# Moving weight and first input loads to time 0, and placing the first one-hot rows with VectorE, in a routed attention followed by a SiLU layer

## The chip, the cores and the metric

The kernel runs on one core of a Trainium2 chip. The metric is the device time in microseconds; the median of three runs of the kernel before is 393.85 us (393.36 to 396.67). The engines named below are TensorE (PE in the profile, with its weight loads as PEld), VectorE (DVE), ScalarE (ACT), GpSimd (POOL) and SyncE (SP, which issues DMAs). GpSimd issues DMAs as well. The profiled run, from which all views are taken, has a span of 390.8 us.

## The reference

Four batches with eight heads each, 768 positions, head dimension 64. Each head has 16 centroids; a query may look only at keys of its own cluster. The result goes, with all heads of a position side by side, through a layer with a SiLU between two matrices.

```python
q, k, v = [4, 8, 768, 64]; centroids = [8, 16, 64]; w_in = [512, 2048]; w_out = [2048, 512]   # float32

c_n = centroids / (norm(centroids) + 1e-6)          # q and k are normalized too: no effect on the argmax
q_assign = argmax(einsum('bhsd,hcd->bhsc', q_n, c_n))
k_assign = argmax(einsum('bhsd,hcd->bhsc', k_n, c_n))
mask = q_assign[:, :, :, None] == k_assign[:, :, None, :]
scores = where(mask, q @ k.T / 8, -1e9)
attn = softmax(scores)
x = (attn @ v).transpose(0, 2, 1, 3).reshape(3072, 512)
h = x @ w_in
out = (h * sigmoid(h)) @ w_out
```

## The kernel before

The kernel works on 16 pairs of heads (`p`), each with three blocks of 256 queries. Of every pair, q and k (`t` = 0 and 1) are loaded, split into two f16 halves (`hl`: the rounded value and the rest), and transposed into `abt`, whose first 64 partitions then hold the rounded values. Pairs 0 to 3 are transposed by TensorE (`turn_pe`), the later ones by a transposing DMA (`turn_dma`). The mask isn't applied to the scores. Instead, the one-hot row of each position's cluster, times 2048, is put under its 64 values, on partitions 64 to 79 of `abt`; a score matmul over 80 partitions then adds 2048 x 2048 where query and key have the same cluster, and the exponential brings the others to zero.

```python
def load(p, t):
    nat = mp.tile([128, 2, NJ * D], f32, name=f"nat{t}", bufs=3)
    nc.sync.dma_start(nat, (q, k)[t][...])

def load_v(p):
    natv = mp.tile([128, 2, NJ * D], f32, name="natv", bufs=2)
    nc.sync.dma_start(natv, v[...])

def cast_v(p):                 # f32 to f16 beside a block of ones, which gives the row sums
    for h in range(2):
        nc.gpsimd.tensor_copy(vts[p % NV][:, :, h, 0:D], natvs[p][:, h]...)

def split(p, t, part, eng=nc.vector): ...       # two VectorE operations of 128x768

def logits(pl):                # q and k against the centroids; wh and wl: two halves of the weights
    for lo, hi in ((0, 512), (512, 768)):
        psL = ps.tile([128, 512], f32, name="psL", tag="moe", bufs=3)
        for n, (w, h) in enumerate(((wh, 0), (wh, 1), (wl, 0), (wl, 1))):
            for a, p in enumerate(pl):
                for t in range(2):
                    g = 64 * a + 32 * t         # 32 rows: 16 of head 0, 16 of head 1
                    nc.tensor.matmul(psL[g : g + 32, 0 : hi - lo], w[:, p % HB, h], ab[:, h, lo:hi], ...)

def route_a(pl):   nc.vector.transpose(lt[0:n, ...], psL...)                  # blocks of 32x32
def route_b(pl):   nc.vector.tensor_reduce(out=mx[0:n], in_=lt, axis=AX.X, op=ALU.max)
def route_c(pl):   nc.vector.tensor_tensor(out=oht..., in0=lt, in1=mx..., op=ALU.is_ge)
def route_d(pl):
    nc.vector.transpose(ohu[0:n], oht)
    nc.vector.tensor_scalar(out=oh[0:n], in0=ohu[0:n], scalar1=OHV, scalar2=None, op0=ALU.mult)
def route_e(pl):               # one DMA for each head and each of q and k
    nc.sync.dma_start(ab[D : D + HC, h, :], oh[g : g + HC, :])
```

After the routing, `qk` makes scores (`st`) and exponentials (`P`), and `pv` multiplies them with v and copies the result to `osb`. The row sums go by DMA to 32 partitions (`z_out`), are inverted by VectorE (`z_recip`), go to DRAM and come back broadcast (`z_bcast`); all three DMAs are issued by GpSimd. `z_mul` makes the input `xt` of the layer, whose units are `unit_a` and `unit_b`. The main loop runs over slots: in each, a third of a unit's scores, the values of the scores of three slots before, what `at(slot, ...)` has put there, and layer units.

```python
def z_out(n):   nc.gpsimd.dma_start(zt, osbs[n][D : D + 1]...)
def z_recip(n):
    nc.vector.reciprocal(rz, zts.pop(n))
    nc.gpsimd.dma_start(rzd..., rz)
def z_bcast(n): nc.gpsimd.dma_start(rzb..., rzs.pop(n).to_broadcast([64, 2 * UQ]))
...
# the start
craw = load_centroids()
for p in range(2):
    for t in range(2):
        load(p, t)
make_identity(nc, ident)
for vt in vts:                                  # six
    nc.gpsimd.memset(vt[:, :, :, D:128], 1.0)
load_v(0)
centroid_norm(craw)
for t in range(2):
    split(0, t, 0, VE); split(0, t, 1)
... # turn_pe of pair 0
for t in range(2):
    split(1, t, 0)
centroid_rest(craw)
logits([0])
for t in range(2):
    load(2, t)
load_v(1)
split(1, 0, 1)
route_a([0]); route_b([0]); route_c([0]); route_d([0]); route_e([0])
cast_v(0)
split(1, 1, 1)
... # turn_pe of pair 1
# the weights: eight DMAs for w_in and eight for w_out, one every second slot; they cast f32 to f16
for n in range(2):
    for r in range(NR):
        wld.append(lambda r=r, o=o: nc.gpsimd.dma_start(win_s[:, r, o], win_v[:, r, o]))
for g in range(NFB // 2):
    wld.append(lambda g=g: nc.gpsimd.dma_start(wout_s[:, 2 * g : 2 * g + 2], wout_v[:, 2 * g : 2 * g + 2]))
...
at(0, lambda: cast_v(1))
at(0, lambda: (load(3, 0), load(3, 1), load_v(2)))
at(3, lambda: load_v(3))
for n, fn in enumerate(wld):
    at(1 + 2 * n, fn)
```

Of the kernel before, what the change touches and what calls it, by code (L numbers as in the profile page):

```python
# [9 lines left out]
f32 = mybir.dt.float32  # L10
f16 = mybir.dt.float16
AF = mybir.ActivationFunctionType
ALU = mybir.AluOpType
AX = mybir.AxisListType
# [3 lines left out]
def kernel(  # L18
# [10 lines left out]
    nc = tc.nc  # L29
    B, H, S, D = q.shape  # L30
    HC = centroids.shape[1]
    DM = moe_w_in.shape[0]
    DF = moe_w_in.shape[1]
    NT = B * S
    NJ = S // 128
    NFB = DF // 128
# [23 lines left out]

    wh = const.tile([128, HB, 2, 32], f16, name="wh")
    wl = const.tile([128, HB, 2, 32], f16, name="wl")
    NV = 6
    vts = [const.tile([128, NJ, 2, 128], f16, name=f"vt{n}") for n in range(NV)]

# [8 lines left out]
    def load(p, t):  # L74
        b, r = divmod(p, HB)
        nat = mp.tile([128, 2, NJ * D], f32, name=f"nat{t}", bufs=3)
        nc.sync.dma_start(nat, (q, k)[t][b, 2 * r : 2 * r + 2].rearrange("h (p j) d -> p h (j d)", j=NJ))
        nats[p, t] = nat

    def load_v(p):  # L80
        b, r = divmod(p, HB)
        natv = mp.tile([128, 2, NJ * D], f32, name="natv", bufs=2)
        nc.sync.dma_start(natv, v[b, 2 * r : 2 * r + 2].rearrange("h (p j) d -> p h (j d)", j=NJ))
        natvs[p] = natv

    def cast_v(p):
        for h in range(2):
            nc.gpsimd.tensor_copy(vts[p % NV][:, :, h, 0:D], natvs[p][:, h].rearrange("p (j d) -> p j d", d=D))

    def split(p, t, part, eng=nc.vector):  # L90
        nat = nats[p, t].rearrange("p h (j d) -> p (h j) d", d=D)
        if part == 0:
            hl = hls[p, t] = mp.tile([128, 2 * NJ, 2, D], f16, name="hl", bufs=3)
            eng.tensor_scalar(out=hl[:, :, 0, :], in0=nat, scalar1=128.0, scalar2=None, op0=ALU.mult)
        else:
            hl = hls[p, t]
            nc.vector.scalar_tensor_tensor(  # L97
                out=hl[:, :, 1, :], in0=nat, scalar=128.0, in1=hl[:, :, 0, :], op0=ALU.mult, op1=ALU.subtract
            )
# [21 lines left out]
    def logits(pl):  # L121
        tl = []
# [5 lines that stand above are left out]
                        g = 64 * a + 32 * t  # L128
                        ab = abts[p][:, t].rearrange("p (h j) c -> p h (j c)", h=2)
                        nc.tensor.matmul(  # L130
                            psL[g : g + 32, 0 : hi - lo], w[:, p % HB, h], ab[:, h, lo:hi], start=(n == 0), stop=(n == 3)
                        )
            tl.append(psL)
        psls[pl[0]] = tl

    def route_a(pl):
        n = 64 * len(pl)
        lt = mp.tile([128, S], f32, name="lt", bufs=1)
        tl = psls.pop(pl[0])
        nc.vector.transpose(lt[0:n, 0:512], tl[0][0:n])  # L140
        nc.vector.transpose(lt[0:n, 512:768], tl[1][0:n, 0:256])
        lts[pl[0]] = lt

    def route_b(pl):
        n = 64 * len(pl)
        lt = lts[pl[0]][0:n].rearrange("p (a c) -> p a c", c=HC)
        mx = mp.tile([128, S // HC], f32, name="mx", bufs=2)
        nc.vector.tensor_reduce(out=mx[0:n], in_=lt, axis=AX.X, op=ALU.max)  # L148
        mxs[pl[0]] = mx

    def route_c(pl):
        n = 64 * len(pl)
        lt = lts.pop(pl[0])[0:n].rearrange("p (a c) -> p a c", c=HC)
        oht = mp.tile([128, S], f16, name="oht", bufs=1)
        nc.vector.tensor_tensor(  # L155
            out=oht[0:n].rearrange("p (a c) -> p a c", c=HC), in0=lt,
            in1=mxs.pop(pl[0])[0:n].unsqueeze(2).to_broadcast([n, S // HC, HC]), op=ALU.is_ge,
        )
        ohts[pl[0]] = oht

    def route_d(pl):
        n = 64 * len(pl)
        ohu = mp.tile([128, S], f16, name="ohu", bufs=1)
        nc.vector.transpose(ohu[0:n], ohts.pop(pl[0])[0:n])  # L164
        oh = mp.tile([128, S], f16, name="oh", bufs=2)
        nc.vector.tensor_scalar(out=oh[0:n], in0=ohu[0:n], scalar1=OHV, scalar2=None, op0=ALU.mult)
        ohs[pl[0]] = oh

    def route_e(pl):
        oh = ohs.pop(pl[0])  # L170
# [3 lines that stand above are left out]
                    g = 64 * a + 32 * t + HC * h  # L174
                    ab = abts[p][:, t].rearrange("p (h j) c -> p h (j c)", h=2)
                    nc.sync.dma_start(ab[D : D + HC, h, :], oh[g : g + HC, :])  # L176


    K = D + HC
# [103 lines left out]
    def centroid_norm(craw):  # L283
        csq = mp.tile([128, D], f32, name="csq")
        nc.vector.tensor_tensor(out=csq, in0=craw, in1=craw, op=ALU.mult)
        nc.vector.tensor_reduce(out=cs, in_=csq, axis=AX.X, op=ALU.add)
        nc.scalar.activation(out=cy, in_=cs, func=AF.Sqrt, bias=zbias, scale=1.0)
        nc.scalar.preload_act_table(AF.Exp)
        newton()

    def centroid_rest(craw):
        newton()
        nc.vector.tensor_scalar(out=cy, in0=cy, scalar1=1e-6, scalar2=None, op0=ALU.add)
        cw = mp.tile([128, 1], f32, name="cw")
        nc.vector.reciprocal(cw, cy)
        cn = mp.tile([128, D], f32, name="cn")
        nc.vector.tensor_scalar(out=cn, in0=craw, scalar1=cw, scalar2=None, op0=ALU.mult)

        chh = mp.tile([128, D], f16, name="chh")
        nc.vector.tensor_copy(chh, cn)  # L300
        ch2 = mp.tile([128, 2, D], f16, name="ch2")
        cl2 = mp.tile([128, 2, D], f16, name="cl2")
        for n in range(2):
            nc.vector.tensor_scalar(out=ch2[:, n, :], in0=chh, scalar1=OHV, scalar2=None, op0=ALU.mult)
        for n in range(2):
            nc.vector.scalar_tensor_tensor(out=cl2[:, n, :], in0=cn, scalar=OHV, in1=ch2[:, n, :], op0=ALU.mult, op1=ALU.subtract)
        for src, dst in ((ch2, wh), (cl2, wl)):
            pt = ps.tile([128, 128], f16, name="pt", tag="moe", bufs=3)
            nc.tensor.transpose(pt, src.rearrange("p n d -> p (n d)"), ident)
            pt4 = pt.rearrange("p (r h c) -> p r h c", h=2, c=HC)  # L310
            for h in range(2):
                nc.vector.tensor_copy(dst[:, :, h, HC * h : HC * h + HC], pt4[:, :, h])


    units = []
# [10 lines left out]
    def at(slot, fn):  # L326
        events.setdefault(slot, []).append(fn)


    nc.vector.memset(zbias, 0.0)  # L330
    nc.vector.memset(bias32, -32.0)
    craw = load_centroids()
    for p in range(2):
        for t in range(2):
            load(p, t)
    make_identity(nc, ident)
    nc.vector.memset(wh, 0.0)
    nc.vector.memset(wl, 0.0)
    for vt in vts:
        nc.gpsimd.memset(vt[:, :, :, D:128], 1.0)  # L340
    load_v(0)
    AC, VE = nc.scalar, nc.vector
    centroid_norm(craw)
    for t in range(2):
        split(0, t, 0, VE)
        split(0, t, 1)
    for t in range(2):
        for h in range(2):
            turn_pe(0, t, h, AC)
    for t in range(2):  # L350
        split(1, t, 0)
    centroid_rest(craw)
    logits([0])
    for t in range(2):
        load(2, t)
    load_v(1)
    split(1, 0, 1)
    route_a([0])
    route_b([0])
    route_c([0])  # L360
    route_d([0])
    route_e([0])
    cast_v(0)
    split(1, 1, 1)
    for t in range(2):
        for h in range(2):
            turn_pe(1, t, h, AC)

    wld = []
    for n in range(2):  # L370
        for r in range(NR):
            o = slice(n * DF // 2, (n + 1) * DF // 2)
            wld.append(lambda r=r, o=o: nc.gpsimd.dma_start(win_s[:, r, o], win_v[:, r, o]))
    for g in range(NFB // 2):
        wld.append(lambda g=g: nc.gpsimd.dma_start(wout_s[:, 2 * g : 2 * g + 2], wout_v[:, 2 * g : 2 * g + 2]))


    def route(pl, x):
# [25 lines left out]
    route([1], 1)  # L404
    front_pe(2, 2)
    front_pe(3, 9)
    at(0, lambda: cast_v(1))
    at(0, lambda: (load(3, 0), load(3, 1), load_v(2)))
    at(3, lambda: load_v(3))
    at(6, lambda: cast_v(2))  # L410
    at(8, lambda: cast_v(3))
    for n, fn in enumerate(wld):
        at(1 + 2 * n, fn)
    for b in range(1, B):
        front([b * HB, b * HB + 1], 36 * b - (3 if b == 1 else 8))
        front([b * HB + 2, b * HB + 3], 36 * b + (4 if b == 1 else 2))
# [88 lines left out]
```

The softmax here doesn't subtract the row's maximum and nothing guards it: scores larger than these inputs give would overflow.

## Time and profile before

| | |
|---|---|
| median of three runs | 393.85 us |
| span of the profiled run | 390.8 us |
| PE busy | 336.5 us (86%) |
| PEld busy | 245.4 us (63%) |
| DVE busy | 248.0 us (63%) |
| ACT busy | 226.0 us (58%) |
| POOL busy | 106.0 us (27%) |
| DMA, issued by SP (q1) | 36.22 MB, 36.7% of 16 engines |
| DMA, issued by GpSimd (q0) | 10.69 MB, 13.5% of 16 engines |

Busy time is the sum of an engine's instructions. A share over the whole span says little here, as the kernel has different stages: a start with loads and routing, a stage with attention alone, and, from about 116 us on, attention and layer units together. The page shows this in forty slices of 9.77 us; each digit is a share of the slice in tenths, PEclk is TensorE's granted clock in tenths of full speed:

```profile
PE   2476965183849999999999999999999999999995
DVE  6827577465554796796755786785845364555661
PEclk9668798588887999999999999999999999999999
DMA  7663589999716179654034598645120111111111
```

TensorE is nearly always busy from the thirteenth slice on. In the seventh to the tenth slice the DMA engines are at 90% or more. The median times from issue to landing differ: 5.7 us for a load of v (384 KB), 5.2 us for a part of w_in and 8.8 us for a part of w_out (256 KB each), 2.0 us for one-hot rows (24 KB).

### The profile page before, as it was taken

Reading aid. Unit: us, or ns where it says so; the run is one execution under the profiler, and the core shown is the slowest. Engines: PE = TensorE matmul, PEld = TensorE weight load, DVE = VectorE, ACT = ScalarE, POOL = GpSimd, SP = SyncE. Lnnn points to the kernel's source line nnn. Section 1 sums busy time; section 2 is a strip of 40 time slices with the busy share of each in tenths; the row PEclk is TensorE's granted clock in tenths of the full one; section 3 lists DMA queues with packets and bytes.
Section 4 is the critical chain, followed back from the end, with each engine's and each line's share of the span. In section 5 each row is a group of like instructions: output and inputs, shape, how many; then the busy total and the mean of one; then the engine's idle time right before and its main releaser. Section 6 shows DMA issues by size and latency. Waiting matters only on the chain.

```text
span 390.8 us, 6883 instructions
## 1 busy us (share of the span) xinstructions
PE 336.5 (86%) x2658; PEld 245.4 (63%) x2658; DVE 248.0 (63%) x464; ACT 226.0 (58%) x255; POOL 106.0 (27%) x204
## 2 busy tenths in 40 slices
PE   2476965183849999999999999999999999999995
PEld 2345644162538877677777776777776777776572
DVE  6827577465554796796755786785845364555661
ACT  5157655054456776574776766665667666663350
POOL 5305162353420314223213133133221313122200
PEclk9668798588887999999999999999999999999999
DMA  7663589999716179654034598645120111111111
GB/s 250 128 200 70 118 164 219 199 243 181 145 45 206 30 190 267 136 138 102 20 118 154 137 245 216 137 101 96 49 68 16 55 42 49 48 43 54 68 42 55
DMA packets 65072, 47.35 MB, mean 121 GB/s; under 512 B 44048, under 2 KB 59408, under 8 KB 65040
## 3 DMA queue, kind: packets, MB, share of 16 engines
q1 hardware_dynamic: 56336, 36.22, 36.7%
q0 software_dynamic: 8704, 10.69, 13.5%
q8 instruction: 21, 0.34, 0.4%
q14 instruction: 11, 0.09, 0.1%
HBM read 33.59 MB, written 6.39 MB: 102 GB/s over the span
## 4 chain that ended last, share of the span: by engine, by line
PE 69%; DVE 12%; DMA 10%; issue 4%; SPq 3%; ACT 2%; DVEq 0%; ACTq 0%
PE ph L246 20%; PE po L260 19%; PE pv L201 14%; PE st L186 13%; DMA abt<-oh 4%; DMA abt<-hl 3%; PE psL L130 3%; DVE hl L97 2%; DMA nat_93<-in_k_dram 2%; DVE oht L155 1%; DVE mx L148 1%; SPq L176 1%; DMA nat_789<-in_q_dram 1%; DVE xt L235 1%; DVE ohu L164 1%
## 5 line engine op out<-in xcount | busy, mean ns | idle before, releaser
L190 ACT ACTIVATE P<-st,bias_70 128x1024 f16<-128x1024 f32 x144 | 158.1, 1115 | 93.8 <-PE st L186 93.1
L186 PE MATMUL st<-abt 80*128 80x256 f16 x576 | 92.2, 284 | 25.8 <-DMA abt<-oh 24.3
L251 DVE SCALAR_TENSOR_TENSOR gt<-tn,ph 128x512 f16<-128x512 f32 x96 | 64.9, 678 | 76.8 <-ACT tn L250 76.5
L246 PE MATMUL ph<-xt,win_s 128*128 128x256 f16 x768 | 99.4, 275 | 2.5 <-DVE lt L140 0.9
L260 PE MATMUL po<-wout_s,gt 128*128 128x512 f16 x384 | 96.0, 379 | 0.0
L250 ACT ACTIVATE tn<-ph,zbias 128x512 f32<-128x512 f32 x96 | 65.6, 684 | 47.4 <-PE ph L246 45.7
L186 PEld LDWEIGHTS <-abt 80*128 80x128 f16 x576 | 56.8, 101 | 46.4 <-DMA abt<-oh 27.0
L246 PEld LDWEIGHTS <-win_s 128*128 128x128 f16 x768 | 75.8, 99 | 15.2 <-issue 3.8
L220 POOL DMA_DIRECT2D rzd<-rz x48 | 25.1, 522 | 158.0 <-DVE rz L218 151.4
L260 PEld LDWEIGHTS <-gt 128*128 128x128 f16 x384 | 37.4, 97 | 28.5
L207 DVE COPY osb<-pv 128x512 f32<-128x512 f32 x48 | 32.5, 676 | 21.2 <-PE pv L201 21.2
L225 POOL DMA_DIRECT2D rzb<-rzd x48 | 25.1, 522 | 68.3 <-DMA rzd<-rz 68.3
L235 DVE TENSOR_TENSOR xt<-osb,rzb 64x256 f16<-64x256 f32 x96 | 40.6, 423 | 3.3 <-DMA rzb<-rzd 2.6
L213 POOL DMA_DIRECT2D zt<-osb x48 | 24.0, 501 | 30.4 <-DVE osb L207 30.1
L201 PE MATMUL pv<-P,vt_77 128*128 128x256 f16 x108 | 17.3, 304 | 5.5 <-DVE osb L207 5.5
L263 DVE TENSOR_SCALAR ot<-po 128x512 f32<-128x512 f32 x24 | 16.1, 669 | 7.8 <-PE po L260 7.8
L113 PE MATMUL ptt<-ident,hl 128*128 128x128 f16 x96 | 9.9, 266 | 11.0 <-DVE hl L97 11.0
L201 PEld LDWEIGHTS <-vt_77 128*128 128x128 f16 x108 | 11.7, 108 | 10.0 <-issue 5.7
L201 PE MATMUL pv<-P,vt_75 128*128 128x256 f16 x108 | 16.1, 289 | 0.0
L116 ACT COPY abt<-ptt 128x768 f16<-128x768 f16 x12 | 9.2, 805 | 11.5 <-PE ptt L113 11.5
L113 PEld LDWEIGHTS <-hl 128*128 128x128 f16 x96 | 8.0, 121 | 12.6 <-DVE hl L97 12.0
L140 DVE STREAM_TRANSPOSE lt<-psL 128x512 f32<-128x512 f32 (+1 forms) x10 | 7.1, 709 | 13.8 <-PE psL L130 13.8
(128 smaller groups left out, 272.3 us busy)
## 6 DMA issues: line engine op xcount, KB each, us to landing
natv<-in_v_dram SPq DMA_DIRECT2D x16, 384.0 KB, 5.7
rzb<-rzd POOLq DMA_DIRECT2D x48, 128.0 KB, 2.9
out_dram<-ot SPq DMA_DIRECT2D x24, 256.0 KB, 2.2
win_s<-in_moe_w_in_dram POOLq DMA_DIRECT2D x8, 256.0 KB, 5.2
wout_s<-in_moe_w_out_dram POOLq DMA_DIRECT2D x8, 256.0 KB, 8.8
abt<-oh SPq DMA_DIRECT2D x64, 24.0 KB, 2.0
zt<-osb POOLq DMA_DIRECT2D x48, 2.0 KB, 2.1
rzd<-rz POOLq DMA_DIRECT2D x48, 2.0 KB, 1.8
```

What stands on the lines that cost most here:

```text
L186: nc.tensor.matmul(st[:, a, h, :], ab[0:K, 1, h, ts(2 * s + a, 128)], ab[0:K, 0, h, ts(u, UQ)], start=True, stop=True)
L190: nc.scalar.activation(out=P, in_=st, func=AF.Exp, bias=bias32, scale=ESC)
L201: nc.tensor.matmul(po[:, h, :], vts[p % NV][:, 2 * s + a, h, :], P[:, a, h, :], start=(s == 0 and a == 0 and h == 0), stop=(s == 2 and a = ...
L207: nc.vector.tensor_copy(osb, po)
L213: nc.gpsimd.dma_start(zt, osbs[n][D : D + 1].rearrange("o h x -> o (h x)").rearrange("o (p i) -> o p i", p=32))
L220: nc.gpsimd.dma_start(rzd.rearrange("o (p i) -> (o p) i", p=32), rz)
L225: nc.gpsimd.dma_start(rzb.rearrange("p h x -> p (h x)"), rzs.pop(n).to_broadcast([64, 2 * UQ]))
L235: nc.vector.tensor_tensor(out=xts[c][D * h : D * h + D, r, :], in0=osb[0:D, h, :], in1=rzb[:, h, :], op=ALU.mult)
L246: nc.tensor.matmul(ph[:, e, :], win_s[:, r, ts(2 * f + e, 128)], xts[c][:, r, :], start=(r == 0), stop=(r == NR - 1))
L250: nc.scalar.activation(out=tn, in_=ph, func=AF.Tanh, bias=zbias, scale=0.5)
L251: nc.vector.scalar_tensor_tensor(out=gts[c][:, 2 * f : 2 * f + 2, :], in0=tn, scalar=1.0, in1=ph, op0=ALU.add, op1=ALU.mult)
L260: nc.tensor.matmul(po, gts[c][:, fc, ts(s, 128)], wout_s[:, fc, :], start=(fc == 0), stop=(fc == NFB - 1))
```

## The change

It has three parts. The loads of q, k and v of pairs 2 and 3 stand earlier in SyncE's order, as early as their buffers allow (three for q, three for k, two for v), and all weights are issued by GpSimd at the start: four DMAs of twice the size for each of the two matrices. GpSimd fills the blocks of ones of only two `vts` before them, and of the other four after. For the first pair the one-hot rows are not put in place by DMA but by four VectorE multiplications, which write to `abt` directly. VectorE can do so because every group of 32 rows now belongs to one head: its 16 logits lie in columns 0 to 15 of each group, for both heads, which takes weights without the shift of 16 for the second head (`w0`). The purpose is to have the first pair ready without the DMAs' latency, and weights and inputs there before they are needed.

```diff
+    w0 = const.tile([128, 2, 32], f16, name="w0")
...
+    oht0 = mp.tile([128, S], f16, name="oht", bufs=1)
+
+    def route_first():
+        tl = []
+        for lo, hi in ((0, 512), (512, 768)):
+            psL = ps.tile([128, 512], f32, name="psL", tag="moe", bufs=3)
+            for i, w in enumerate((wh, wl)):
+                for h in range(2):
+                    for t in range(2):
+                        g = 64 * h + 32 * t
+                        ab = abts[0][:, t].rearrange("p (h j) c -> p h (j c)", h=2)
+                        nc.tensor.matmul(
+                            psL[g : g + 32, 0 : hi - lo], w0[:, i] if h else w[:, 0, 0], ab[:, h, lo:hi],
+                            start=(i == 0), stop=(i == 1),
+                        )
+            tl.append(psL)
+        lt = mp.tile([128, S], f32, name="lt", bufs=1)
+        nc.vector.transpose(lt[:, 0:512], tl[0])
+        nc.vector.transpose(lt[:, 512:768], tl[1][:, 0:256])
+        l3 = lt.rearrange("p (a c) -> p a c", c=32)[:, :, 0:HC]
+        mx = mp.tile([128, S // 32], f32, name="mx0")
+        nc.vector.tensor_reduce(out=mx, in_=l3, axis=AX.X, op=ALU.max)
+        oht = oht0
+        nc.vector.tensor_tensor(
+            out=oht.rearrange("p (a c) -> p a c", c=32)[:, :, 0:HC], in0=l3,
+            in1=mx.unsqueeze(2).to_broadcast([128, S // 32, HC]), op=ALU.is_ge,
+        )
+        ohu = mp.tile([128, S], f16, name="ohu", bufs=1)
+        nc.vector.transpose(ohu, oht)
+        for h in range(2):
+            for t in range(2):
+                g = 64 * h + 32 * t
+                ab = abts[0][:, t].rearrange("p (h j) c -> p h (j c)", h=2)
+                nc.vector.tensor_scalar(
+                    out=ab[D : D + HC, h, :], in0=ohu[g : g + HC, :], scalar1=OHV, scalar2=None, op0=ALU.mult
+                )
...  (centroid_rest, for each half of the weights)
+            nc.vector.tensor_copy(w0[:, i, 0:HC], pt4[:, 0, 1])
...  (the start)
+    load_v(0)
     make_identity(nc, ident)
     nc.vector.memset(wh, 0.0)
     nc.vector.memset(wl, 0.0)
-    for vt in vts:
+    nc.vector.memset(w0, 0.0)
+    nc.vector.memset(oht0, 0.0)
+    for vt in vts[0:2]:
         nc.gpsimd.memset(vt[:, :, :, D:128], 1.0)
-    load_v(0)
     centroid_norm(craw)
+    for r in range(NR):
+        nc.gpsimd.dma_start(win_s[:, r], win_v[:, r])
+    for g in range(NFB // 4):
+        nc.gpsimd.dma_start(wout_s[:, 4 * g : 4 * g + 4], wout_v[:, 4 * g : 4 * g + 4])
...
-    for t in range(2):
-        split(1, t, 0)
-    centroid_rest(craw)
-    logits([0])
     for t in range(2):
         load(2, t)
     load_v(1)
+    for t in range(2):
+        load(3, t)
+    split(1, 0, 0)
+    split(1, 1, 0)
+    centroid_rest(craw)
     split(1, 0, 1)
-    route_a([0])
-    route_b([0])
-    route_c([0])
-    route_d([0])
-    route_e([0])
+    route_first()
     cast_v(0)
+    for vt in vts[2:]:
+        nc.gpsimd.memset(vt[:, :, :, D:128], 1.0)
+    cast_v(1)
+    load_v(2)
+    load_v(3)
     split(1, 1, 1)
...  (wld, its two loops, and the events of load(3), load_v(2), load_v(3), cast_v(1) and wld are gone)
```

More of the change, by code (lines that the diff above doesn't have):

```diff
@@ L306, in centroid_rest @@
             nc.vector.scalar_tensor_tensor(out=cl2[:, n, :], in0=cn, scalar=OHV, in1=ch2[:, n, :], op0=ALU.mult, op1=ALU.subtract)
-        for src, dst in ((ch2, wh), (cl2, wl)):
+        for i, (src, dst) in enumerate(((ch2, wh), (cl2, wl))):
             pt = ps.tile([128, 128], f16, name="pt", tag="moe", bufs=3)
@@ L327, in at @@
         events.setdefault(slot, []).append(fn)
+    AC, VE = nc.scalar, nc.vector
     nc.vector.memset(zbias, 0.0)
@@ L338 @@
     nc.vector.memset(wl, 0.0)
-    for vt in vts:
+    nc.vector.memset(w0, 0.0)
+    nc.vector.memset(oht0, 0.0)
+    for vt in vts[0:2]:
         nc.gpsimd.memset(vt[:, :, :, D:128], 1.0)
-    load_v(0)
-    AC, VE = nc.scalar, nc.vector
     centroid_norm(craw)
+    for r in range(NR):
+        nc.gpsimd.dma_start(win_s[:, r], win_v[:, r])
+    for g in range(NFB // 4):
+        nc.gpsimd.dma_start(wout_s[:, 4 * g : 4 * g + 4], wout_v[:, 4 * g : 4 * g + 4])
     for t in range(2):
-        split(0, t, 0, VE)
+        split(0, t, 0)
         split(0, t, 1)
@@ L367 @@
             turn_pe(1, t, h, AC)
[L369 to L375, printed above, removed]
     def route(pl, x):
@@ L406 @@
     front_pe(3, 9)
-    at(0, lambda: cast_v(1))
-    at(0, lambda: (load(3, 0), load(3, 1), load_v(2)))
-    at(3, lambda: load_v(3))
     at(6, lambda: cast_v(2))
     at(8, lambda: cast_v(3))
-    for n, fn in enumerate(wld):
-        at(1 + 2 * n, fn)
     for b in range(1, B):
```

## The prediction

> **What bounds the kernel now.** I read four views in this order: the page's forty slices, the busy times cut into stages, the chain of waits over the first 75 us, and single lines of the timeline. Windows first; columns are the stretch, its length, busy time (and instructions) of PE, PEld, DVE, ACT and POOL, then the PE clock, the DMA share and GB/s:
> ```profile
> 0.00:22.60 22.60, 8.29 (x66) 5.92 (x66) 14.26 (x38) 8.82 (x11) 9.05 (x19) 0.78 0.71 187
> 22.60:50.00 27.40, 23.93 (x194) 16.65 (x195) 17.28 (x28) 18.11 (x19) 7.87 (x16) 0.81 0.46 119
> 50.00:102.00 52.00, 28.86 (x216) 19.79 (x214) 32.17 (x57) 22.07 (x22) 20.06 (x35) 0.77 1.18 208
> 120.00:391.00 271.00, 263.53 (x2088) 194.37 (x2085) 175.40 (x324) 168.41 (x196) 63.63 (x125) 1.00 0.38 102
> ```
> After 120 us PE is busy 264 of 271 us: that part is matmul work, and the change leaves it alone. Before that PE waits for 14 us in the prologue, 3.5 us in the next stage, and 23 us between 50 and 102, where the DMA share is above 1: the DMA engines are full. So what can be won lies in the first 120 us, and mostly between 50 and 102.
>
> The chain of waits (start, length, what), with the steps that the change touches:
> ```profile
> 2.67 6.06 DMA nat_93<-in_k_dram
> ...
> 17.50 0.36 DVE oh L166
> ...
> 18.70 3.88 DMA abt<-oh
> 22.59 0.04 issue
> 22.63 2.01 PE st L186 x8
> ```
> The first score matmul needs the whole front: four loads of q and k (the last lands at 8.73), the routing on DVE until 17.86, then the one-hot DMAs, which land at 22.6, 4.7 us later. In the full stage the same chain holds one-hot DMAs (53.25 to 56.93), a load (74.72 to 79.79) and transposing DMAs (79.79 to 92.81); the list of waits has PE waiting 24.3 us for one-hot DMAs, 11.6 us in the longest case (64.4 to 76.0).
>
> **What the Trainium skill says.** "DMA: Bandwidth & Descriptors", section "Issuing engines are not separate DMA queues": DMAs of SP and GpSimd run on the same 16 engines and interleave. The trace agrees: between 39 and 41 us, with loads and weights both in flight, the rate is 231 GB/s, between 402 for loads alone (10 to 11 us) and 135 for weights alone (16 to 17 us). The same page, section "Queues, rings and completion order", says that an engine takes the work of one queue in ring order and goes round robin between queues. For the order within GpSimd's queue I looked at a small DMA of row sums (zt, line 213) issued just after a weight load (line 373):
> ```profile
> 48.88 0.59 POOL L373 DMA_DIRECT2D win_s<-in_moe_w_in_dram  x1
> 49.44 0.52 POOL L213 DMA_DIRECT2D zt<-osb  x1
> DMA to landing us min/median/max: 3.8/3.8/3.8
> ```
> The last line is that zt's. It lands at 53.2; the weight load ahead of it (4.2 us) at 53.1. Behind another (87.69) it took 8.5 us, and with none ahead (30.68) 1.6 us. So a small transfer of this queue waits until the weights issued before it have landed.
>
> **The change, part by part.**
>
> *1. One-hot rows by VectorE.* Removed: from the end of oh at 17.86 to the first matmul at 22.63, 4.77 us, and oh itself, 0.36. Added: four multiplications of 16x768. The line-166 one, 64x768 in the same types, took 0.35; the cost follows the 768 columns and not the partitions (a 64x512 and a 128x512 transpose both take 0.71), so 4 x 0.37 = 1.5 us. The groups of 32 columns now hold 16 logits of one head, so maximum and comparison run over 384 columns in place of 768: 0.95 and 0.96 should become about 0.5 each, 0.9 saved. Two further weight copies (about 0.15 each): +0.3. The 16 logits matmuls stay as many. Sum: 4.77 + 0.36 + 0.9 - 1.5 - 0.3 = **4.2 us** earlier.
>
> *2. All weights at time 0.* Nothing is removed; 16 DMAs of 256 KB (as written in f16) become 8 of 512 KB, issued by GpSimd from about 2.6 us on, after two of the 0.73 us memsets. What one costs: three of them alone, 15.5 to about 21.6 us with 98 KB of one-hot rows, give (6.1 - 0.5)/3 = 1.87; one alone between 33.4 and 36.0 gives 1.75. With 1.8 for win and, an estimate, 2.0 for wout, whose rows are half as long: 8 x 1.8 + 8 x 2.0 = **30 us of all DMA engines**.
> Effect on the first loads: traffic from about 4.2 us (the issue at 13.89 moved its first bytes at 15.5). By then the loads have about 600 KB of the 1605 KB that end with pair 1's k. From then on they share: 38 to 43 us shows 231 = f x 380 + (1 - f) x 135, f = 0.4, so 152 GB/s in place of 380. (1605 - 600)/152 = 6.6 us, and 1.2 to land: about 12.1 in place of 8.73, **3.4 us later**. The DVE has both first-half splits of pair 1 ahead of the centroid work, so this is on the path. Parts 1 and 2 together: first score matmul at 22.63 - 4.2 + 3.4 = 21.8.
>
> *3. The row sums behind the weights.* When the queue is empty: 4.2 + what is left of 12 loads, (12 x 393 - 600) KB/380 = 10.8 us, + 30 + 1 of one-hot rows = 46; overlap of two queues (5.0 us for 5.8 us' worth between 38 and 43) takes perhaps 2 off, landing adds 1.2: about **45 to 46 us**. All zt of the first units wait for that. On DVE, in order, the first one is waited for here:
> ```profile
> 37.05 0.23 DVE L218 RECIPROCAL rz<-zt 32x16 f32<-32x16 f32 x1
> 42.37 0.69 DVE L207 COPY osb<-pv 128x512 f32<-128x512 f32 x1 [5.08 <-PE pv L201]
> ```
> Today rz has its data and DVE then idles 5 us for pv. With zt landing at 45.5 the copy starts at 45.8 in place of 42.4: **+3.4 us**, which swallows what part 1 had won (the two don't add: the wait sets the time, whatever came before).
>
> *4. The DMA engines from 50 to 102 us.* This is where I expect the gain. What runs there today, by DMA time: 8 transposes at 2.3 (the one from 141.5 to 143.8) = 18.4; 10 loads at 393 KB/380 = 10.3; 8 wout and the last two win = 19.6; one-hot rows and row sums about 5; sum 53 of 52 us. Take the weights away and a third is free. By stall: the one-hot DMAs at 53.25 land after 2.0 (as at 36.00) and not 3.68: 1.7. The long one: SP is held by a transposing DMA until 68.3 while oh is ready at 66.8, and then landing takes 5.2 in place of 2.0: 1.5 + 3.2 = 4.7. The 5.5 us before 96.8, where DVE waits 4.4 for a transposing DMA: 4.5. Two waits of 1.2 and 1.1 for transposed halves in front of the logits (84.2, 101.6): 2. Sum 12.9. The chain also holds DVE work and fixed latencies that move up into the space, so I count 75%: **-9.7 us**.
>
> Sum: 3.4 - 9.7 = -6.3 us; 393.85 - 6.3 = 387.5. Part 2 may cost less (the larger descriptors may run faster and the queue empty sooner), so I move it one down: **386.5**.
>
> **Rivals.** *A: the first loads starve.* If the engines divide by packets and weight packets are the longer, the loads get nearer 20% than 40%: (1605 - 600)/76 = 13 us, so k lands at 18.6 and the first matmul comes near 28. For it: each row of win is 4096 B in f16 after the change against 1536 B of a load. Against: the 40% were measured with 2048 B rows. The queue would empty no later, as the total is the same, so it costs less than it seems: 28 + (42.4 - 22.6) = 47.8 in place of 45.8 for the copy, some 389. *B: the weights cost more than 30 us*, and the wait of part 3 lasts to 52: 6.5 more, 393, no change. Or they cost 24, the wait vanishes into the idle 5 us, and the time is near 383. *C: the weights were hidden anyway*, and the 50 to 102 stage is a chain of DVE, SP and landing latencies: then only +3.4 remains, 397. For it: DVE is busy 32 of 52 us there. Against: the share of 1.18, and landings of 7 us for one-hot rows that take 2.0 elsewhere. *D: the front sets everything*, its 4.2 us go through, the loads don't suffer and the row sums aren't late: 380 with part 4. Against: the queue order shown above.
>
> **Range and chances.** Centre 386.5, with 2 to 3 us of doubt in part 3 and 5 in part 4. Range 378 to 396. Faster by 2% means under 386.0, just below the centre: 0.46. Slower by 2% means over 401.7 and needs A and C together: 0.09. The rest, 0.45.
>
> **What would show it.** Part 1: four DVE copies near 0.37 us and the first score matmul within 0.2 us of the last; the reduction near 0.5. Part 2: pair 1's k landing near 12; under 10 or over 16 breaks it. Part 3: the first rz of DVE standing after an idle of some 8 us that ends with the DMA of zt, and the last weight landing just before it; if it starts near 36 without a wait, the queue was empty sooner. Part 4: the DMA share between 50 and 100 clearly under 1, one-hot rows landing in 2 to 3 us, the 11.6 us stall under 8. PE after 120 us as busy as now; if not, the time is elsewhere and all of this is beside the point.

## The result, and the profile after

The changed kernel takes 384.66 us in the median of four runs (381.46 to 387.58), the kernel before 395.26 in the runs beside it; the ratio is 0.970, with a 95% interval of 0.961 to 0.980. The prediction had said 386.5, which is 7.4 us under the 393.85 that it started from; the medians here are 10.6 apart. The time is near where it was expected, but only the last of the four terms behind it is.

Two profiles of the changed kernel were taken. The lines shown here are of the second (span 382.1 us). Between the first scores and the third osb copy TensorE's granted clock was 1.00 in it and 0.75 in the first, where that stage was 4 us longer; why it differs from one execution to the next was not found out. In this stage the second profile is the exception: the kernel before has 0.76 there, the profiles of the experiments below 0.72 to 0.86. For this stage the first profile is the one to compare with theirs. The other stages agree within 0.4 us, the end, which holds no change, within 1.3.

First the busy times by stage, in the stretches shown of the kernel before (length, busy time of PE, PEld, DVE, ACT and POOL, PE clock, DMA share, GB/s):

```profile
0.00:22.60 22.60, 5.73 (x49) 4.16 (x50) 10.16 (x37) 5.82 (x7) 8.83 (x19) 1.00 0.95 228
22.60:50.00 27.40, 20.29 (x191) 15.41 (x189) 19.27 (x32) 18.52 (x20) 9.04 (x15) 1.00 0.74 178
50.00:102.00 52.00, 37.74 (x317) 27.06 (x314) 41.05 (x73) 30.02 (x30) 19.74 (x35) 0.84 0.76 168
```

The DMA share of the stretch from 50 to 102 us went from 1.18 to 0.76, and PE is busy for 37.7 us of it in place of 28.9: the work of the same stretch gets done sooner. But the first stretch has become worse: 49 matmuls (5.7 us of PE) in place of 66 (8.3), with the DMA engines full (0.95 in place of 0.71). The list of waits has PE waiting for one-hot DMAs 16.6 us in all, 8.8 in the longest case (24.3 and 11.6 before). The line of the kernel before comes first (in all, times, longest):

```profile
PE st L186 <- DMA abt<-oh: 24.3, 10, 11.6
PE st L226 <- DMA abt<-oh: 16.6, 8, 8.8
```

Where the front lost its time is seen in the chain of waits up to the first scores (start, length, what):

```profile
2.68 14.64 DMA nat<-in_k_dram
...
26.11 0.35 DVE abt L214
26.48 0.97 DVE hl L99
27.49 1.46 PE ptt L115 x12
28.95 1.07 PE st L226 x5
```

The load of pair 1's k took 14.6 us in place of 6.1. And the one-hot copies, with which the chain was to end, are followed by a split and twelve transposes before the first scores.

Five marks in the timeline cut every run into the same pieces: the first split of pair 1's k on VectorE (its load has landed), the first score matmul (st), the third copy of attention values (osb; the first row sums are waited for just before it), the first layer matmul (ph), and the end of the span. Times in us, one profile each:

| kernel | k of pair 1 | to first score | to third osb | to first ph | to the end | span |
|---|---|---|---|---|---|---|
| before | 8.8 | 13.8 | 19.7 | 73.8 | 274.6 | 390.8 |
| changed, first profile | 17.8 | 11.3 | 20.9 | 62.3 | 273.3 | 385.5 |
| changed, second profile | 17.4 | 11.3 | 16.7 | 62.2 | 274.5 | 382.1 |

The change moved three pieces: k came 8.6 to 8.9 later, the way from there to the scores got 2.5 shorter, and the piece from the third osb to the first layer matmul 11.5 to 11.6 shorter. The end is within 1.4 us of what it was. The span of the kernel before, 390.8, is of one of its faster executions (392.84 us by device time, where the median is 395.26), so the spans differ by less (5.3 and 8.7) than the medians.

### The profile page after: what moved, and what is told of

Read it like the earlier page. It is cut to its first block, busy times and chain, and to the rows that moved or that the text cites. A ratio compares the mean times of both kernels' runs of the same rounds, so it can differ in the third digit from the quotient of the medians.

```text
span 385.5 us, 6875 instructions
## 1 busy us (share of the span) xinstructions
PE 333.6 (87%) x2658; PEld 244.2 (63%) x2658; DVE 250.2 (65%) x471; ACT 225.9 (59%) x255; POOL 103.4 (27%) x196
## 3 DMA queue, kind: packets, MB, share of 16 engines
q0 software_dynamic: 8064, 10.69, 11.6%
## 4 chain that ended last, share of the span: by engine, by line
PE 70%; DVE 13%; DMA 10%; issue 4%; ACT 2%; SPq 1%; DVEq 0%; ACTq 0%
PE ph L286 20%; PE po L300 19%; PE st L226 14%; PE pv L241 13%; DMA nat_95<-in_k_dram 4%; DMA abt<-hl 4%; PE psL L132 3%; DMA abt<-oh 2%; DVE hl L99 2%; DVE xt L275 1%; DVE hl L96 1%; DVE oht L157 1%; ACT tn L290 1%; DVE osb L247 1%; DVE ohu L166 1%
## 5 line engine op out<-in xcount | busy, mean ns | idle before, releaser
L286 PEld LDWEIGHTS <-win_s 128*128 128x128 f16 x768 | 75.3, 98 | 14.9 <-issue 3.8
L260 POOL DMA_DIRECT2D rzd<-rz x48 | 25.1, 523 | 155.5 <-DVE rz L258 155.0
L265 POOL DMA_DIRECT2D rzb<-rzd x48 | 25.1, 522 | 64.0 <-DMA rzd<-rz 60.0
L253 POOL DMA_DIRECT2D zt<-osb x48 | 24.0, 499 | 24.5 <-DVE osb L247 24.3
L118 ACT COPY abt<-ptt 128x768 f16<-128x768 f16 x12 | 9.2, 806 | 21.4 <-PE ptt L115 21.4
L241 PE MATMUL pv<-P,vt_78 128*128 128x256 f16 x108 | 16.1, 289 | 1.3 <-DVE osb L247 1.3
L241 PE MATMUL pv<-P,vt_76 128*128 128x256 f16 x108 | 16.1, 289 | 0.0
L241 PE MATMUL pv<-P,vt_79 128*128 128x256 f16 x108 | 15.6, 283 | 0.0
L132 PE MATMUL psL<-abt,wh 128*32 128x512 f16 (+1 forms) x120 | 11.3, 350 | 4.3 <-DMA abt<-hl 3.6
```

Of the source, the lines that this page charges most:

```text
L241: nc.tensor.matmul(po[:, h, :], vts[p % NV][:, 2 * s + a, h, :], P[:, a, h, :], start=(s == 0 and a == 0 and h == 0), stop=(s == 2 and a = ...
L253: nc.gpsimd.dma_start(zt, osbs[n][D : D + 1].rearrange("o h x -> o (h x)").rearrange("o (p i) -> o p i", p=32))
L260: nc.gpsimd.dma_start(rzd.rearrange("o (p i) -> (o p) i", p=32), rz)
L265: nc.gpsimd.dma_start(rzb.rearrange("p h x -> p (h x)"), rzs.pop(n).to_broadcast([64, 2 * UQ]))
L286: nc.tensor.matmul(ph[:, e, :], win_s[:, r, ts(2 * f + e, 128)], xts[c][:, r, :], start=(r == 0), stop=(r == NR - 1))
```

## The experiments

All ratios are against the kernel before on the same chip, with 95% intervals. Pieces are those of the table above.

### The changed kernel again

No edit.

> The changed kernel once more, for a second profile and a ratio on the same chip as the other runs. If its time is what the first measurement gave, the ratio is near 0.970. The first profile had pair 1's k landing at 17.6 us, the first score matmul at 29.1 and the first layer matmul at 112.3. If the landing of k is set by how the queues divide the engines, it comes back within 1 us; if it was an accident of that run, it comes near 12, as predicted, and the time falls by some 5 us.

386.06 us, ratio 0.975 (0.967 to 0.982). The split of pair 1's k started at 17.4 us, within 0.4 of the first profile: the delay is not an accident of one run.

### Two of the three parts, one at a time

The kernel before, with only the weights moved to time 0:

```diff
-    for vt in vts:
+    for vt in vts[0:2]:
         nc.gpsimd.memset(vt[:, :, :, D:128], 1.0)
     load_v(0)
     centroid_norm(craw)
+    for r in range(NR):
+        nc.gpsimd.dma_start(win_s[:, r], win_v[:, r])
+    for g in range(NFB // 4):
+        nc.gpsimd.dma_start(wout_s[:, 4 * g : 4 * g + 4], wout_v[:, 4 * g : 4 * g + 4])
...  (the other four memsets behind cast_v(0); wld and its events gone)
```

> The kernel before with nothing changed but the weights: all eight DMAs at time 0, behind two of the memsets. Theory (weights starve the first loads, and pay it back between 50 and 102 us): k of pair 1 lands near 17.6, the first score matmul comes near 33 (22.6 + 9 + 1 for one-hot DMAs among weights), the first layer matmul near 115; time within 1% of before, ratio 0.98 to 1.00. Rival (the weights' place is the whole gain): ratio near 0.97. Rival (the weights' place costs, and the one-hot rows by VectorE brought the gain): over 1.00.

393.06 us, ratio 0.996 (0.993 to 0.998). K at 16.2, first score at 31.2, first layer matmul at 115.1 against 116.2. The pieces are 14.9, 22.6 and 61.4: the last is 12.4 us shorter than before, and 7.4 of later k, 1.1 of slower one-hot DMAs among weights, and 2.9 up to the third osb take nearly all of it back. So the weights' new place alone is worth about half a per cent (0.2 to 0.7).

The kernel before, with only the one-hot rows of the first pair placed by VectorE:

```diff
-    logits([0])
...
-    route_a([0]); route_b([0]); route_c([0]); route_d([0]); route_e([0])
+    route_first()
...  (w0, oht0 and their memsets as in the change)
```

> The kernel before with the one-hot rows of the first pair placed by VectorE, weights issued as before. As predicted for this part: first score matmul 4.2 us earlier, near 18.4. What the profile after suggests: 2.4 earlier only, near 20.2, as TensorE has the transposes of pair 1's k in front of the first scores, and these wait for a split behind the one-hot copies. In time: if what is won in the front goes through to the end, 2 to 4 us less, ratio 0.990 to 0.995; if a wait further on takes it, 1.000.

390.41 us, ratio 0.985 (0.979 to 0.992). K at 9.4, and 11.5 us from there to the first score in place of 13.8: 2.3 won, not 4.2. The piece from the third osb to the layer is 74.4 and not touched by this part. The ratio is better than the 0.990 to 0.995 expected, but the profile has the first layer matmul only 1.2 us earlier and the span only 2.4 shorter; two of the six executions, at a mean clock of 0.955 and 0.960 in place of 0.938 to 0.943, took 386.4 us, and why is not shown.

The third part, the earlier loads of pairs 2 and 3, was not run on its own. The last piece doesn't need it, as the weights alone bring it to 61.4. Whether it helps elsewhere stays open: the two ratios multiplied give 0.981, the whole change has 0.970 and 0.975, and the intervals overlap.

### How much the weights hold up the full stage

The kernel before with the weights not loaded; GpSimd fills the two tiles with zeros in slot 0. This leaves out the weights; every matmul is still done.

```diff
+    at(0, lambda: nc.gpsimd.memset(win_s.rearrange("p r f -> p (r f)"), 0.0))
+    at(0, lambda: nc.gpsimd.memset(wout_s.rearrange("p c d -> p (c d)"), 0.0))
...  (wld and its events gone)
```

> The kernel before without any load of weights: GpSimd fills both weight tiles with zeros instead, in slot 0. It leaves out the weights, so its output is zero; the work of every engine but the DMAs is the same. It bounds what freeing the DMA engines can bring. Theory (the 50 to 102 stage is bound by the full DMA engines): DMA share there from 1.18 to below 0.9, first layer matmul 9 to 13 us earlier, ratio 0.967 to 0.977. Rival (that stage is a chain of VectorE, SP and landing latencies, and the weights were hidden): first layer matmul under 4 us earlier, ratio above 0.99.

396.13 us, ratio 1.006 (1.003 to 1.009), as the rival had it, but for another reason. The piece from the third osb to the layer is 62.5, 11.3 us shorter. The front, however, is 12.8 us longer between k and the first scores. The timeline of VectorE and that of GpSimd at the same time (start, length, engine, line):

```profile
10.95 14.14 DVE L297 TENSOR_SCALAR cn<-craw,cw 128x64 f32<-128x64 f32 x1
```
```profile
11.25 6.93 POOL L364 MEMSET win_s<- 128x8192 f16 x1
18.11 6.93 POOL L365 MEMSET wout_s<- 128x8192 f16 x1
```

An operation of 64 columns, 0.25 to 0.5 us elsewhere, lasts until GpSimd's second memset is over. The zeros had slowed the kernel, so the run was made again with the zeros written by VectorE where it idles (behind the last split of pair 1).

```diff
+    nc.vector.memset(win_s.rearrange("p r f -> p (r f)"), 0.0)
+    nc.vector.memset(wout_s.rearrange("p c d -> p (c d)"), 0.0)
```

> As the run without weights before, but the zeros are written by VectorE, behind the last split of pair 1, where it idles for 8 us; GpSimd writes none. It leaves out the weights, so its output is zero. In the first such run a 128x64 operation of VectorE took 14.1 us beside GpSimd's two memsets of 6.9 us. If the memsets held it up, it takes 0.3 to 0.5 here, the first score matmul comes near 21, the third osb copy near 41, and the 62 us from there to the first layer matmul give 103: ratio 0.960 to 0.970. If the weights were hidden, the stage from the third osb copy to the first layer matmul is back at 74 and the ratio at 0.99 to 1.00.

383.11 us, ratio 0.970 (0.964 to 0.976). The same operation took 0.42 us, the first scores came at 21.7, and the last piece took 61.1 us. The third osb came at 44.7 and not at 41: VectorE's two memsets (3.5 us each, with waits, until 28.4) ran 2 us over the idle time they were put in. So without any weight traffic the piece is 61 us long; the changed kernel has it at 62: nearly everything that weights cost there is gone. These runs take away two things at once, the weights' bytes and their place ahead of the row sums in GpSimd's queue. Which of them counted was not separated; that the longest waits there (one-hot rows, transposes) are for DMAs that SyncE issues speaks for the bytes.

### Why the first loads starve

The changed kernel with w_in in pieces of 1024 or 512 columns, still ahead of GpSimd's other work, the same bytes:

```diff
-    for r in range(NR):
-        nc.gpsimd.dma_start(win_s[:, r], win_v[:, r])
+    for n in range(2):                                 # 4 in the second run
+        for r in range(NR):
+            o = slice(n * DF // 2, (n + 1) * DF // 2)  # DF // 4
+            nc.gpsimd.dma_start(win_s[:, r, o], win_v[:, r, o])
```

> The same with eight DMAs of 1024 columns, the pieces of the kernel before: rows of 4096 B read. By the same rule the loads get 1536/(1536 + 4096) = 27%, about 110 of 405 GB/s, so 1005 KB take 9.1 us from 4.2 on and k lands near 14.5; the first score matmul near 26, ratio 0.965 to 0.972. If my prediction's 40% held for rows of this length, k would land near 12.1.

> The changed kernel with the w_in weights still at time 0, but in 16 DMAs of 512 columns: each row read is 2048 B in place of 8192 B, the same bytes in all. If an engine takes turns row by row, the loads, with rows of 1536 B, get 1536/(1536 + 2048) = 43% of what is read and not 1536/(1536 + 8192) = 16%: k of pair 1 lands near 11.5 us in place of 17.6, the first score matmul comes near 23, ratio 0.955 to 0.967. If the turns don't follow the rows, k stays near 17 and the ratio near 0.975.

With 1024 columns 384.34 us, ratio 0.974 (0.968 to 0.980); with 512, 382.49 us, 0.971 (0.963 to 0.979). The splits of pair 1's q and k on VectorE start when their loads have landed; first 1024, then 512 columns:

```profile
10.44 0.56 DVE L96 TENSOR_SCALAR hl<-nat 128x768 f16<-128x768 f32 x1 [3.04 <-DMA nat<-in_q_dram]
14.34 0.56 DVE L96 TENSOR_SCALAR hl<-nat 128x768 f16<-128x768 f32 x1 [3.35 <-DMA nat<-in_k_dram]
```
```profile
10.80 0.56 DVE L96 TENSOR_SCALAR hl<-nat 128x768 f16<-128x768 f32 x1 [3.36 <-DMA nat<-in_q_dram]
13.01 0.56 DVE L96 TENSOR_SCALAR hl<-nat 128x768 f16<-128x768 f32 x1 [1.65 <-DMA nat<-in_k_dram]
```

The load of k behind that of q takes 1.06 us before, 5.8 in the changed kernel (rows of 8192 B read), 3.9 with rows of 4096 B, and 2.2 with 2048 B. If each engine takes one row of each queue in turn, a load with rows of 1536 B takes 1 + R/1536 times as long: 6.7, 3.9 and 2.5 us. The middle value fits, the outer ones are 11 to 14% under it. The profile's count of DMA packets shows the turns themselves. Between the splits of q and of k, q0 (GpSimd's weights) and q1 (SyncE's loads) moved (packets, MB as written, share of 16 engines; rows of 8192, 4096 and 2048 B read):

```profile
q0 software_dynamic: 269, 0.97, 84.0%
q1 hardware_dynamic: 272, 0.39, 21.8%
```
```profile
q0 software_dynamic: 288, 0.52, 72.0%
q1 hardware_dynamic: 293, 0.43, 36.1%
```
```profile
q0 software_dynamic: 255, 0.23, 62.4%
q1 hardware_dynamic: 256, 0.37, 53.2%
```

One packet of each queue in turn, whatever its length; a packet here is a row (but for 44 to 48 of 4 B in each of the three stretches). So the shares follow the rows. The bytes outstanding are no rival, though with 512 columns they were fewer: GpSimd issued eight DMAs by 7 us and the others only as earlier ones landed, until 24.8, but the turns were one to one all the same.

K came where expected with 1024 columns (14.3 for 14.5) and 1.5 us late with 512 (13.0 for 11.5), because q was already late. The load of q doesn't follow the rule: it comes 6.0, 4.7 and 5.0 us after the one before it, with the shortest rows no sooner than with the middle ones (1.75 in the kernel before). Between 6 and 10 us all engines together moved 195 to 238 GB/s (bytes as written) in these runs and 350 before; why is not shown. The first scores moved with k (25.7 and 24.4 in place of 28.8), while both ratios came out a little above the ranges expected. Of the 4.4 us that k gained with 512 columns the span shows 2.1 against the second profile and 5.5 against the first; the piece up to the third osb (21.4 at a clock of 0.74, against 16.7 at 1.00 and 20.9 at 0.75) is what makes the two differ.

### Weights behind the first loads

The changed kernel with the eight weight DMAs issued after the cast of the first v:

```diff
     centroid_norm(craw)
-    (the weights)
...
     cast_v(0)
+    (the weights)
     for vt in vts[2:]:
         nc.gpsimd.memset(vt[:, :, :, D:128], 1.0)
```

> The changed kernel with one thing moved: GpSimd issues the eight weight DMAs behind the cast of the first v, so that they start when the loads of pairs 0 and 1 have landed. Theory (at time 0 the weights starve the loads of pair 1): k of pair 1 lands near 8.7 us in place of 17.6, the first score matmul comes near 20.5 in place of 29, and what stands between the third osb copy and the first layer matmul stays at 62 us. The weights still end near 38, so the first row sums wait for them: third osb copy near 41 to 43, first layer matmul near 104; ratio 0.955 to 0.968. Rival (the front is not what sets the time, as the wait for row sums or the one-hot DMAs take it back): first layer matmul over 107, ratio 0.972 or more.

380.52 us, ratio 0.965 (0.960 to 0.970). K at 9.7, and 61.8 us from the third osb to the layer: the early loads and the short last piece are had together. The first score came at 23.7, though, 3 us later than expected. VectorE's one-hot copies took 3.88 us in place of 1.53, beside GpSimd's four memsets and the cast behind them:

```profile
17.53 3.88 DVE L214 TENSOR_SCALAR abt<-ohu 16x768 f16<-16x768 f16 x4
```
```profile
16.82 2.87 POOL L409 MEMSET vt<- 128x768 f16 x4
19.54 1.29 POOL L90 CAST vt<-natv 128x384 f16<-128x384 f32 x2
```

The next two runs put all six memsets back to the start. In the second of them w_out follows later.

```diff
-    for vt in vts[0:2]:
+    for vt in vts:
         nc.gpsimd.memset(vt[:, :, :, D:128], 1.0)
...  and, in the second run, w_in alone behind cast_v(0), and
+    for g in range(NFB // 4):
+        at(5 + 3 * g, lambda g=g: nc.gpsimd.dma_start(wout_s[:, 4 * g : 4 * g + 4], wout_v[:, 4 * g : 4 * g + 4]))
```

> The changed kernel with the weights behind the cast of the first v, as in the run before, and all six blocks of ones filled at the start again. In that run the four one-hot copies took 3.88 us in place of 1.54, beside four memsets of GpSimd (16.8 to 19.7 us). If the memsets held them, they take about 1.6 here and the first score matmul comes 2.3 us earlier, near 21.4; in time 1 to 2 us less than that run, ratio 0.955 to 0.965. If the weight traffic held them, they stay at 3.9 and so does the time. The row sums might then wait for the last weight, as I had predicted for the changed kernel: a wait of 1 to 3 us in front of the first reciprocal.

> As the run with early ones, but only w_in is issued behind the cast of the first v; the four DMAs of w_out follow one by one behind the row sums of the first four units (slots 5 to 14), where the DMA engines are idle in the changed kernel (46 to 60 us, share 0.1 to 0.3). They are small stretches of 2 to 4 us, so the row sums behind them are up to 3 us late, inside the 4 slots that they have. If the full engines between 20 and 38 us hold up the one-hot rows and loads of pairs 1 and 2, this is 1 to 3 us faster than the run with early ones; if only the loads of pairs 0 and 1 mattered, the same within 1 us.

380.51 us, 0.963 (0.957 to 0.970), and 380.54 us, 0.964 (0.954 to 0.974). In the first, the copies took 1.62 us with the weights still in flight, so the memsets had held them. The first score came at 20.3, 3.4 earlier than in the run before (2.3 from the copies, the rest from k at 8.5); the time is unchanged all the same. The next piece took 1.9 back (22.1 in place of 20.2): PE waited 2.4 us for pair 1's one-hot DMAs, which took 2.8 to 4.3 us among the weights, and the clock there was 0.73 in place of 0.84. The last piece took another 0.8, and the span is 1.1 us shorter. The wait for row sums that I had predicted for the changed kernel appears here, but costs nothing, as VectorE then idles another 4.7 us for the values that the third osb copies:

```profile
37.33 0.24 DVE L258 RECIPROCAL rz<-zt 32x16 f32<-32x16 f32 x1 [0.93 <-DMA zt<-osb]
42.31 0.69 DVE L247 COPY osb<-pv 128x512 f32<-128x512 f32 x1 [4.74 <-PE pv L241]
```

These row sums were issued at 29.06 and landed 8.2 us later, 0.2 after the last weight (at 37.13). With w_out later the third osb came at 40.6 in place of 42.3, and the stage behind it was 63.6 in place of 62.6: most of what is taken out of one piece is put into the other. Up to the layer the two differ by 0.8 us, and the medians by 0.03, inside the 1 us expected if only the loads of pairs 0 and 1 mattered.

### The transposes in front of the first scores

```diff
-    split(1, 1, 1)
-    for t in range(2):
-        for h in range(2):
-            turn_pe(1, t, h, AC)
+    for h in range(2):
+        turn_pe(1, 0, h, AC)
+    at(0, lambda: (split(1, 1, 1), turn_pe(1, 1, 0, AC), turn_pe(1, 1, 1, AC)))
```

> The changed kernel with TensorE's transposes of pair 1's k moved behind the first four score matmuls (and the split that feeds them behind the one-hot copies, as before). Theory (the prediction's 4.2 us for the one-hot part became 2 because the first scores stand behind these transposes): the first score matmul follows the last one-hot copy within 0.3 us, 2.2 us earlier than in the changed kernel, near 26.8. In time 0 to 2 us less, as the route of pair 1 still needs the transposes: ratio 0.969 to 0.975 against before. If the first score still waits, something else held it.

384.37 us, ratio 0.975 (0.969 to 0.981). The first score came at 25.4, 8.4 us behind k in place of 11.3, while the copies were still going on. So the transposes had held it. Nothing of that is seen in the time: the second group of scores and the routing of pair 1 need the same transposes, and the first values (pv) came at 32.5 against 33.1.

## Why the prediction was right, and where it wasn't

The four terms, as predicted and as measured in the second profile against the kernel before (the first profile in brackets). The third row contains the first two; the span is the sum of the last three:

| step | predicted | measured |
|---|---|---|
| 1, one-hot rows by VectorE | -4.2 | -2.5 (-2.5) |
| 2, first loads beside the weights | +3.4 | +8.6 (+8.9) |
| third osb copy, set by the row sums' wait | +3.4 | +3.1 (+7.6), no wait |
| 4, third osb to the first layer matmul | -9.7 | -11.6 (-11.5) |
| rest | 0 | -0.2 (-1.4) |
| span | -6.3 | -8.7 (-5.3) |

**Part 1: what VectorE and the DMAs cost was right, the order of TensorE was left out.** The reduction and comparison took 0.55 and 0.56 us, the four copies 1.53. What failed is the step "from the end of oh to the first matmul", which took the whole DMA wait as won. In the kernel before, the split of pair 1's k and its twelve transposes ran inside that wait:

```profile
18.77 1.46 PE L113 MATMUL ptt<-ident,hl 128*128 128x128 f16 x12 [3.39 <-DVE hl L97]
22.63 0.39 PE L186 MATMUL st<-abt 80*128 80x256 f16 x1 [2.40 <-DMA abt<-oh]
```

With the wait gone they stand on the path, 2.3 us from the last copy to the first score. The run with only this part has the same 2.3 us of gain.

**Part 2: the mechanism was right, the share was mis-sized.** I took f = 0.4 for the loads from a stretch in which loads and two weight DMAs overlapped for part of the time, and with rows of 4096 B read (the 2048 B in the text are the f16 side). The 231 GB/s put down to 38 to 43 us are those of 39 to 41; the longer stretch has 251. The rows of the changed kernel are 8192 B, and the loads get 1.06/5.8 = 18%. This is rival A, which had k at 18.6; it landed near 17.4.

**Part 3: the order of the queue was right, but the wait set nothing.** Two sizes were wrong. The DMA engines were nearly empty at 37.3 us and not at 46. They were full for 33.1 us from 4.2 on, of which the loads' bytes make 10.8 at their own rate: 22 us for the weights, not 30. The two queues overlap by more than the 2 us allowed for (share 1.09 to 1.23 between 30 and 36); this fits, but no run tests it. And the front was late: the first row sums were issued at 36.1 and landed at 38.8, 0.2 after the last weight, and their reciprocal at 42.4 waited for nothing. The wait does come in three runs, 0.9 us with early ones, 1.6 and 2.8 with w_in in pieces of 1024 and 512 columns; each time VectorE then idles another 4.3 to 4.7 us for pv before the third osb. So in every profile the third osb waited for pv, and never for row sums. That it lay within 0.3 us of the predicted place in the second profile is luck: late loads at a fast clock gave what I had put down to the row sums. The first profile, at the usual clock, has it 4.1 us later than predicted.

**Part 4 held,** somewhat over its size. The DMA share is 0.76, and the piece is about 1 us longer than the one without any weights (61.1). Of its stalls, the long one fell from 11.6 to 8.8, and the wait of pv for the osb copy from 5.5 to 1.2. One-hot DMAs took 1.8 to 1.9 us in the first profile where none was in their way; those of the long stall still took 3.5 to 4.5 in the first profile and 4.1 to 5.8 in the second, in place of 6.6 to 7.3. The stall fell under 8, as forecast, only in the first (7.3). The waits for transposed halves in front of the logits fell only in part. PE's busy time in the piece went from 44.3 to 43.3 us for the same matmuls, at a clock of 0.85 in place of 0.82.

So the front, where the change was to help, lost 3 to 8 us up to the third osb, and the stage that no part of it touches by name won 11.6. Rival C, that the weights were hidden, is out by the two runs without weights. That the total came out near is partly luck: parts 1 and 2 had the first scores 6.9 us too early, and 4.3 of that was made up by a wait (third osb at 45.8 in place of 21.8 + 19.7 = 41.5) that I had expected and that didn't set the time.

## What to carry to other kernels

Moving transfers to time 0 doesn't make them free: look at what else is in flight then, and issue bulk loads behind the first loads that something waits for. Here that one move took the changed kernel from 384.66 and 386.06 us in its two measurements to 380.52. That is 4.1 and 5.5 us, or 0.5 and 1.0% by the ratios (0.970 and 0.975 to 0.965), whose intervals overlap; both later runs that kept the move gave 380.5 again. Three further changes to the front gave nothing that the times show, as the next waits took back most of each. When a wait is taken away, list what other engines did during it; it may be the next link of the chain.

## What the runs showed of the hardware that was not expected

*Rows decide how two DMA queues share.* A load of 393 KB with rows of 1536 B took 1.06, 2.2, 3.9 and 5.8 us beside nothing and beside weight rows of 2048, 4096 and 8192 B read. The Trainium skill ("DMA: Bandwidth & Descriptors", section "Queues, rings and completion order") says that an engine goes round robin between queues, a whole packet at a time. The runs agree: 256 to 255, 293 to 288 and 272 to 269 packets. They show besides that a packet here was one row, so that the length of the rows sets what a turn is worth, for rows of these lengths.

*A GpSimd memset holds VectorE.* An operation of 64 columns took 14.14 us beside two memsets of 6.93, and 0.42 without them; four copies took 3.88 us beside memsets and a cast, and 1.62 without the memsets. The skill ("SBUF — State Buffer", section "Who interferes with whom") says that GpSimd and some VectorE operations share a pair of ports, which one of them holds for its whole instruction. The runs agree, and show that VectorE can lose more than one instruction's time: the operation started at 10.95, while a cast of GpSimd's still ran (to 11.31), and both memsets went ahead of it. Reductions were not seen to wait: one of 128x384 took 0.55 us inside GpSimd's memsets (22.4 to 25.1 us in the second profile) and 0.55 without.
